# An attention kernel with a gated MLP: reciprocals stored in token order, and the first query product one slot earlier

## The chip, the cores and the metric

The kernel runs on one core of one Trainium2 chip. The metric is device time in microseconds of one execution; a span is the time from the first to the last instruction in the profile. Engine names are those of the profile: PE is TensorE's matmul, PEld its weight load, DVE VectorE, ACT ScalarE, POOL GpSimd, SP the SyncE queue that issues almost all DMAs here.

## The reference

```python
xn = layernorm(x)                       # x: 2048 tokens x 512
# A: attention, 32 heads of 128, keys and values from a cache of 2048 positions
q = (xn @ wq).reshape(B, Sq, H, Dh).transpose(0, 2, 1, 3)
p = softmax(q @ k_cache^T * Dh**-0.5)
s = (p @ v_cache).transpose(0, 2, 1, 3).reshape(B, Sq, H * Dh) @ wo
# B: shifted channel groups and an MLP
h = gelu(layernorm(xn) @ w1);  hs = shift(h) @ w2;  x1 = xn + hs
b = x1 + gelu(layernorm(x1) @ w3) @ w4
out = x + s * silu(b)
```

All arrays are bf16. The weights are wq 512 x 4096, wo 4096 x 512, w1 and w2 512 x 512, w3 512 x 1792, w4 1792 x 512.

## The kernel before

The MLP branch comes first (some 120 us); its end is interleaved with the first attention units. Attention is cut into 128 units: a unit is one head (`hh` within its group of four) for one quarter of the queries (512 tokens, `qt`), and eight groups `g` of four heads follow one another. Within a group the order is `qt`, then `hh`. Each unit has 8 slots (`SPU`), and one loop over `n` = 8 x unit + slot (line 921 on) writes down by hand, slot by slot, what is issued; `pin` keeps that order on every engine. `u` is the unit and `p` the slot (0 to 7).

**Scores and values.** In each slot `s_slot` makes the scores of two blocks of 128 keys against the 512 queries (two matmuls into one of two psS buffers), and ACT takes the exponential of both in one instruction (L423). `pv_run` follows ten slots behind (`LAG`): two matmuls per slot add values weighted by exponentials into `ps_o`, 128 head channels x 512 tokens, one of two psO buffers. A unit's value matmuls thus begin in slot 2 of the next unit, and need the buffer that the quotient (`norm`, L496) of the unit two before it has read.

**Softmax sums.** VectorE adds the exponentials of all keys in bf16 (`add_first` L429, `add_next` L434, `fold` L438, `fold_last` L442) down to 128 partitions x 512 tokens. For the first 124 units (`TURN`) the sums over the 128 partitions go this way: in slot 3 of the next unit SP issues a DMA transpose of that tile (`turn`, L467), so that partition `p` holds tokens `j*128 + p`, `j` = 0 to 3; in slot 0 of the unit after that VectorE adds along the free axis (`turned_sums`, L472) and takes the reciprocal (`turned_recip`, L478), 128 x 4 numbers; SP stores them to a small DRAM tile `dr` (L480); in slot 1 SP reads `dr` back, broadcast to all 128 partitions (`bcast`, L484), as `rb`, 128 x 512; in slot 7 VectorE multiplies `ps_o` by `rb` and writes `oT` (`norm`, L496). In `dr` the number of token `j*128 + p` stands at place `4p + j`. So `rb` and `oT` are in that order too: the quotient reads `ps_o` with a step of 128 numbers, and the projection's weight load picks 128 tokens of one block out of `oT` with a step of 4 (`o_cols`). The other four units have no such order: three of them use `sums`, whose `dr` is in token order, and the last is divided in halves in another way.

**Projection.** When the four heads of a group are done for a `qt`, `norm_queue` puts four token blocks on a list; each following unit takes one: four matmuls, one per head, into one psX buffer (tag `xm`), in the slots that `at_wo` names, and in the fifth of these VectorE adds the result to `sacc` (`wo_post`, L560).

**Queries.** From unit 16 on the queries of two heads are made together (a pair, `v` and `v + 1`) in seven products of two matmuls over 256 columns each, instead of eight (Strassen's way, in Winograd's form), during the 16 slots of units `v - 2` and `v - 1`. Products 1, 6, 2 go to one psX buffer (tag `xa`), products 7, 5, 4, 3 to the next one made from the same bank. ACT copies the buffer's first half after products 1 and 2 (`q_take` 0 and 1, L393), VectorE does the sums (`q_part`: L400, L403, L405, L407). `steps` names the slot of each, counted from the first slot of unit `v - 2`. In a slot the order is: scores, values, product, `q_take`, later the projection's matmul. The differences of weights that the products need come from `w_sum` (L361).

The slots that the change touches are set in these lines, with `FIRST` = 16 and `LAST` = 124:

```python
        for k, n in ((1, 1), (6, 2), (2, 5), (7, 8), (5, 9), (4, 12), (3, 13)):
            steps[a + n].append((product, v, k))
        for i, n in enumerate((1, 5)):
            steps[a + n].append((q_take, v, i))
...
        if FIRST - 2 <= u < LAST:
            at_wo = ([0, 3, 4, 6, 7], [0, 2, 3, 6, 7], [3, 4, 5, 6, 7], [0, 2, 3, 6, 7])[u % 4]
```

Of the kernel before, what the change touches and what calls it, by code (L numbers as in the profile page):

```python
# [10 lines left out]
FP32 = mybir.dt.float32  # L11
# [6 lines left out]
def kernel(  # L18
# [15 lines left out]
    nc = tc.nc  # L34
    P = nc.NUM_PARTITIONS
# [9 lines left out]
    QT = Sq // 512  # L45
# [5 lines left out]
    HG = 4  # L51
# [10 lines left out]
    pin = tc.keep_in_program_order  # L62

    def pool(name, bufs=1, space=None, **kw):
        if space is not None:
            kw["space"] = space
        return tc.tile_pool(name=name, bufs=bufs, **kw)
# [26 lines left out]
    drp = ent(pool("drp", 4, bass.MemoryType.DRAM))  # L94
# [16 lines left out]
    def mm(out, lhsT, rhs, start, stop, **kw):  # L111
# [9 lines left out]
        out=ident[:], in0=diag[:], scalar1=0.0, scalar2=None, op0=ALU.is_equal))  # L121
# [7 lines left out]
    TURN = range(NU - HG)  # L129
# [185 lines left out]
    def q_mm(u, dcs, tag="xa"):  # L315
        g, qt, hh = units[u]
        if dcs[0] == 0:
            st[u] = dict(psq=psX.tile([P, 512], FP32, tag=tag, name="ps_q"))
        for dc in dcs:
            mm(st[u]["psq"][:], wqs[g * HG + hh][:, dc, :],  # L320
               xnT[:, dc, qt * 512:(qt + 1) * 512], dc == 0, dc == DC - 1)
# [90 lines left out]
    def s_slot(u, p):  # L412
        g, qt, hh = units[u]
        s = st[u]
        sps = psS.tile([P, 2, 512], FP32, name="ps_s")
        for j in range(2):
            kc = 2 * p + j
            kv = kTs[g * HG + hh].rearrange("d (i p j) -> d i j p", p=P, j=KJ)
            mm(sps[:, j, :], kv[:, kc // KJ, kc % KJ, :], s["qT"][:], True, True)
        if p % 2 == 0:  # L420
            s.setdefault("pT", []).append(pB.tile([P, 4, 512], BF16, tag="pT", bufs=6, name="pT"))
        jj = 2 * (p % 2)
        pin(nc.scalar.activation(  # L423
            out=s["pT"][-1][:, jj:jj + 2, :], in_=sps[:], func=ACT.Exp, scale=SCALE))
# [7 lines left out]
    def add_next(u, i):  # L432
        a = st[u]["acc"]
        pin(nc.vector.tensor_tensor(out=a[:], in0=a[:], in1=st[u]["pT"][i][:], op=ALU.add))  # L434

    def fold(u):
        a = st[u]["acc"]
        pin(nc.vector.tensor_tensor(out=a[:, 0:2, :], in0=a[:, 0:2, :], in1=a[:, 2:4, :], op=ALU.add))  # L438

    def fold_last(u):  # L440
        a = st[u]["acc"]
        pin(nc.vector.tensor_tensor(out=a[:, 0, :], in0=a[:, 0, :], in1=a[:, 1, :], op=ALU.add))  # L442
# [26 lines left out]
    def turned_sums(u):  # L469
        s = st[u]  # L470
        sm = s["sm"] = smp.tile([P, 4], FP32, name="sm")
        pin(nc.vector.tensor_reduce(out=sm[:], in_=s["tT"][:], axis=mybir.AxisListType.X, op=ALU.add))  # L472

    def turned_recip(u):
        s = st[u]
        sm = s["sm"]
        rc = smp.tile([P, 4], FP32, name="rc")
        pin(nc.vector.reciprocal(out=rc[:], in_=sm[:]))  # L478
        s["dr"] = drp.tile([P, 4], FP32, name="dr")
        pin(nc.sync.dma_start(out=s["dr"][:], in_=rc[:]))  # L480

    def bcast(u):
        st[u]["rb"] = pB.tile([P, 512], FP32, tag="rb", bufs=2, name="rb")
        pin(nc.sync.dma_start(  # L484
            out=st[u]["rb"][:], in_=st[u]["dr"][:].rearrange("p j -> (p j)").partition_broadcast(P)))

    def norm(u):
        g, qt, hh = units[u]
        s = st.pop(u)
        if hh == 0:  # L490
            oTs[(g, qt)] = pB.tile([P, HG, 512], BF16, tag="oT", bufs=2, name="oT")
        o, rb, to = s["o"][:], s["rb"][:], oTs[(g, qt)][:, hh, :]
        if u in TURN:
            o = o.rearrange("k (j p) -> k p j", j=4)
            rb, to = (x.rearrange("k (p j) -> k p j", j=4) for x in (rb, to))
        pin(nc.vector.tensor_tensor(out=to, in0=o, in1=rb, op=ALU.mult))  # L496

    wo_box = {}
# [5 lines left out]

    def o_cols(g, qt, hh, ts):
        o = oTs[(g, qt)][:, hh, :]
        if (g * QT + qt) * HG + hh in TURN:
            return o.rearrange("k (p j) -> k j p", j=4)[:, ts, :]
        return o[:, ts * P:(ts + 1) * P]

    def wo_mm(g, t, hhs, tag="xm"):
# [28 lines left out]
    def pay():  # L540
        while owed:
            y_out(*owed.popleft(), nc.sync)
# [317 lines left out]
    def pv_run(n):  # L860
        while pv_at[0] <= n - LAG:
            pv_slot(*divmod(pv_at[0], SPU))
            pv_at[0] += 1
# [11 lines left out]
    def wo_slot(part, n, each=2, **kw):  # L875
        gg, t = wo_todo[0]
        if part < HG // each:
            wo_mm(gg, t, tuple(range(part * each, (part + 1) * each)), **kw)
            return
        wo_todo.popleft()  # L880
        wo_post(gg, t, n)
        if gg == NG - 1 and t % 4 < 3 and t + 1 not in fin and t // 4 not in LATE:
            fin_load(t + 1)
# [5 lines left out]
    first, third = {}, {}  # L889
    for v in pairs:  # L890
        a = (v - 2) * SPU
        for k, n in ((1, 1), (6, 2), (2, 5), (7, 8), (5, 9), (4, 12), (3, 13)):
            steps[a + n].append((product, v, k))
        for i, n in enumerate((1, 5)):
            steps[a + n].append((q_take, v, i))
        steps[a + 14].append((q_part, v, 3))
        first[v - 2] = v
        third[v - 1] = (v,)

    def fold_at(u):  # L900
        return 1 if u in third else 0

    def run_steps(n, which):
        for fn, v, k in steps.get(n, ()):
            if fn is which:
                fn(v, k)
# [4 lines left out]
    for h in range(HG, H, 2):  # L911
        u = (h // HG) * QT * HG + (-4, -2)[h % HG // 2]
# [8 lines left out]
    for n in range(UB * SPU):  # L921
        u, p = divmod(n, SPU)
        extra = len(wo_todo) > 1 and u in (2 * HG, 2 * HG + 1)
        if p == 0 and wo_box:
            wo_slot(4, n, each=1)
        s_slot(u, p)
        pv_run(n)
        for v, dcs in q_plan.get(n, ()):
            q_mm(v, dcs)
        run_steps(n, product)  # L930
        run_steps(n, q_take)
        if p == 0 and 1 <= u:
            if u - 2 in TURN:
                turned_sums(u - 2)
                turned_recip(u - 2)
            add_next(u - 1, 3)
        if p == 1 and u - 2 in TURN:
            bcast(u - 2)
        if p == fold_at(u) and 1 <= u:
            for v in third.get(u, ()):  # L940
                q_part(v, 1)
            fold(u - 1)
            for v in third.get(u, ()):
                q_part(v, 2)
            if u != UA and u not in first:
                fold_last(u - 1)
        if p == 2 and u in first:
            q_part(first[u], 0)
            fold_last(u - 1)
        if p == 3 and u - 1 in TURN:  # L950
            turn(u - 1)
        if p == 0:
            twice = extra
        if twice and p < 3:
            wo_slot(p, n, tag="xa")
        for v, k in ((u + 1, 3), (u + 2, 7)):
            if p == k and "psq" in st.get(v, ()) and (k == 3) == (v > FIRST):
                q_copy(v)
        if u - 2 in TURN:
            norm_p, sum_p, wo_p, each = 7, 5, 3, 1  # L960
        else:
            norm_p, sum_p, wo_p, each = 4, 5, 4, 1
        at_wo = [wo_p + i for i in range(HG // each + 1)]
        if FIRST - 2 <= u < LAST:
            at_wo = ([0, 3, 4, 6, 7], [0, 2, 3, 6, 7], [3, 4, 5, 6, 7], [0, 2, 3, 6, 7])[u % 4]
        if p == norm_p and 2 <= u and not u - 2 in TURN:
            norm_queue(u - 2)
        if p == sum_p and 1 <= u and u - 1 not in TURN:
            sums(u - 1)
        if p == sum_p + 1 and 1 <= u and u - 1 not in TURN:  # L970
            bcast(u - 1)
        if u == UA and p in (1, 2, 3):
            wo_slot(p - 1, n)
            if p == 3:
                fold_last(u - 1)
        if p in at_wo and wo_todo and pS is not None and (p == at_wo[0] or wo_box):
            wo_slot(at_wo.index(p), n, each=each)
        if p == norm_p and u - 2 in TURN:
            norm_queue(u - 2)
        run_steps(n, q_part)  # L980
        if p == 4:
            add_first(u)
        if p == 6:
            add_next(u, 2)
        pay()
        held_mm(n)
        for fn in todo.pop(n, ()):
            fn()
        if pS is None and not held:
            right.close()  # L990
            pS = right.enter_context(pool("pS", side="right", reuse_waits="tile"))
# [3 lines left out]
    n = UB * SPU  # L995
# [27 lines left out]
    def pv_to(k):  # L1023
# [29 lines left out]
        out=diag[:], in0=diag[:], scalar1=0.0, scalar2=None, op0=ALU.is_equal))  # L1053
# [98 lines left out]
```

## Time and profile before

| | us |
|---|---|
| median of 3 runs | 1241.74 |
| lowest and highest run | 1241.14, 1241.91 |
| the profiled execution | 1240.9 |
| its span | 1239.1 |
| TensorE's granted clock | 1.000 of full speed |
| ACT busy, DVE busy | 1112.6, 1030.3 |
| 16 DMA engines: share of the span that queue q1's packets took | 41.1% |

How to read the rows that follow. A row of a group gives the line, the engine, the operation, output and inputs, shapes and count; then busy time in us and the mean of one in ns; then the engine's idle time just before, and what ended it. A row of the timeline gives the start in us, the length in us, and the same names, with "xN" where neighbouring instructions of one kind are merged; matmuls are pipelined, so the length of a merged pair includes the draining of the last, and the pace is read from starts. A row of the chain gives start, length and what. A row of a window gives its ends, its length, and the busy time and count of PE, PEld, DVE, ACT and POOL, then the clock, the share of the DMA engines and GB/s. A row of DMA issues gives the kind, the count, the size and the median time in us from issue to landing. A row of waits gives who waited for whom, the total in us, how many times and the longest.

### The profile page before, as it was taken

To read this page: it belongs to the slowest core of one execution; us is meant where nothing else is said; L and a number is where in the kernel's file an instruction comes from. 1 tells how busy PE (TensorE), PEld (TensorE's weight loads), DVE (VectorE), ACT (ScalarE), POOL (GpSimd) and SP (SyncE) were. 2 spreads that over 40 slices of the span, in tenths; PEclk is the share of its full clock that TensorE was granted. 3 is DMA by queue.
4 is the path that set the end of the run, shared out by engine and by line. 5 is a ranking of instruction groups with operands and counts; after the bars stand their busy time and mean duration, and the time that the engine had idled before them with its cause. 6 is when DMAs were issued, how large, how long until landed. Compare 5 with 4: busy or idle time off the path is not lost.

```text
span 1239.1 us, 17537 instructions
## 1 busy us (share of the span) xinstructions
PE 1233.0 (100%) x6267; PEld 644.2 (52%) x6267; DVE 1030.3 (83%) x1647; ACT 1112.6 (90%) x1237; POOL 26.7 (2%) x75
## 2 busy tenths in 40 slices
PE   9999999999999999999999999999999999999998
PEld 6444444455555555555555555555555555555555
DVE  7712778898888888888889888888889999999997
ACT  6345999899999999999999999999999999999996
POOL 5300000000000000000000000000000000000000
PEclk9999999999999999999999999999999999999999
DMA  8760112554334423353243423443345435543332
GB/s 175 171 148 21 31 39 65 98 97 91 66 76 100 109 53 82 86 112 84 57 90 95 111 55 69 100 103 75 71 87 107 102 65 86 103 103 69 77 80 67
DMA packets 244056, 107.75 MB, mean 87 GB/s; under 512 B 194816, under 2 KB 227712, under 8 KB 243968
## 3 DMA queue, kind: packets, MB, share of 16 engines
q1 hardware_dynamic: 243408, 106.17, 41.1%
q8 instruction: 49, 0.80, 0.3%
q14 instruction: 39, 0.32, 0.1%
q10 hardware_dynamic: 560, 0.46, 0.1%
HBM read 67.50 MB, written 2.36 MB: 56 GB/s over the span
## 4 chain that ended last, share of the span: by engine, by line
PE 95%; DVE 3%; DMA 1%; ACT 1%; issue 0%; POOL 0%; DVEq 0%; ACTq 0%
PE ps_s L112 39%; PE ps_o L112 37%; PE ps_q L112 8%; PE ps_wo L112 8%; PE ps_m L112 2%; DVE acc L434 1%; ACT pT L423 1%; DMA rb<-dr 0%; DMA tT<-acc 0%; DVE sm L472 0%; DVE oT L496 0%; DMA xin<-in_A_x_dram 0%; PE ps_oh L112 0%; DMA dr<-rc 0%; DVE y L1014 0%
## 5 line engine op out<-in xcount | busy, mean ns | idle before, releaser
L423 ACT ACTIVATE pT<-ps_s 128x1024 bf16<-128x1024 f32 x1016 | 1019.8, 1025 | 54.4 <-PE ps_s L112 24.8
L112 PE MATMUL ps_s<-qT,kT 128*128 128x512 bf16 (+1 forms) x2064 | 609.0, 377 | 0.0
L112 PE MATMUL ps_o<-pT,vb 128*128 128x512 bf16 x1984 | 589.9, 379 | 0.0
L434 DVE TENSOR_TENSOR acc<-acc,pT 128x2048 bf16<-128x2048 bf16 x254 | 307.0, 1209 | 54.6 <-ACT pT L423 54.1
L112 PEld LDWEIGHTS <-kT 128*128 128x128 bf16 x2064 | 232.7, 113 | 147.4 <-issue 2.4
L112 PEld LDWEIGHTS <-vb 128*128 128x128 bf16 x1984 | 194.0, 98 | 216.9 <-issue 0.3
L429 DVE TENSOR_TENSOR acc<-pT 128x2048 bf16<-128x2048 bf16 x127 | 155.4, 1224 | 43.0 <-ACT pT L423 41.9
L112 PE MATMUL ps_wo<-wo_h,oT 128*128 128x512 bf16 x496 | 186.2, 379 | 0.0
L438 DVE TENSOR_TENSOR acc<-acc 128x1024 bf16<-128x1024 bf16 x127 | 87.4, 688 | 2.5
L496 DVE TENSOR_TENSOR oT<-ps_o,rb 128x512 bf16<-128x512 f32 x127 | 86.6, 682 | 1.5 <-DMA rb<-dr 1.2
L472 DVE TENSOR_REDUCE sm<-tT 128x4 f32<-128x512 bf16 x124 | 83.9, 677 | 2.0 <-DMA tT<-acc 2.0
L112 PEld LDWEIGHTS <-oT 128*128 128x128 bf16 x528 | 59.1, 112 | 49.5 <-issue 0.6
L112 PEld LDWEIGHTS <-wc 128*128 128x128 bf16 x440 | 42.9, 98 | 57.9 <-issue 12.7
L560 DVE TENSOR_TENSOR sacc<-ps_wo,sacc 128x512 f32<-128x512 f32 x96 | 65.7, 684 | 0.0
L112 PEld LDWEIGHTS <-wq_h 128*128 128x128 bf16 x398 | 38.9, 98 | 46.3
L112 PE MATMUL ps_q<-xnT,wq_h 128*128 128x256 bf16 (+1 forms) x288 | 61.1, 298 | 0.4 <-DVE sacc L548 0.4
L407 DVE TENSOR_TENSOR qT<-ps_q,tq 128x512 bf16<-128x512 f32 x55 | 38.0, 692 | 23.7 <-PE ps_q L112 23.5
L442 DVE TENSOR_TENSOR acc<-acc 128x512 bf16<-128x512 bf16 x127 | 53.0, 417 | 0.5
L293 ACT ACTIVATE h2T<-ps_s 128x1024 bf16<-128x1024 f32 x28 | 28.7, 1024 | 25.9 <-PE ps_s L112 25.9
L112 PEld LDWEIGHTS <-w_sb 128*128 128x128 bf16 x368 | 33.6, 98 | 29.6
L112 PE MATMUL ps_s<-xn2T,w_sb 128*128 128x512 bf16 x224 | 48.8, 379 | 0.0
L112 PE MATMUL ps_q<-xs,wc 128*128 128x256 bf16 x246 | 46.8, 271 | 0.0
(102 smaller groups left out, 586.4 us busy)
## 6 DMA issues: line engine op xcount, KB each, us to landing
rb<-dr SPq DMA_DIRECT2D x127, 256.0 KB, 3.9
vb<-in_A_v_cache_dram SPq DMA_DIRECT2D x62, 256.0 KB, 3.0
wq_h<-in_A_wq_dram SPq DMA_DIRECT2D x32, 128.0 KB, 3.1
wo_h<-in_A_wo_dram SPq DMA_DIRECT2D x32, 128.0 KB, 2.7
w_sb<-in_B_w_dram SPq DMA_DIRECT2D x8, 256.0 KB, 5.1
kT<-in_A_k_cache_dram SPq DMA_TRANSPOSE x128, 2.8
xl<-in_A_x_dram SPq DMA_DIRECT2D x16, 128.0 KB, 3.0
dr<-rc SPq DMA_DIRECT2D x127, 2.0 KB, 1.4
```

Source lines behind the costliest of these rows:

```text
L112: pin(nc.tensor.matmul(out=out, lhsT=lhsT, rhs=rhs, start=start, stop=stop, **kw))
L293: pin(nc.scalar.activation(out=h2[c, f][:], in_=ps[:], func=ACT.Gelu_apprx_tanh))
L407: pin(nc.vector.tensor_tensor(out=s["q"][:, 1:3, :], in0=ps[:], in1=s["u"][:].unsqueeze(1).to_broadcast([P, 2, 256]), op=ALU.add))
L423: pin(nc.scalar.activation(out=s["pT"][-1][:, jj:jj + 2, :], in_=sps[:], func=ACT.Exp, scale=SCALE))
L429: pin(nc.vector.tensor_tensor(out=s["acc"][:], in0=s["pT"][0][:], in1=s["pT"][1][:], op=ALU.add))
L434: pin(nc.vector.tensor_tensor(out=a[:], in0=a[:], in1=st[u]["pT"][i][:], op=ALU.add))
L438: pin(nc.vector.tensor_tensor(out=a[:, 0:2, :], in0=a[:, 0:2, :], in1=a[:, 2:4, :], op=ALU.add))
L442: pin(nc.vector.tensor_tensor(out=a[:, 0, :], in0=a[:, 0, :], in1=a[:, 1, :], op=ALU.add))
L472: pin(nc.vector.tensor_reduce(out=sm[:], in_=s["tT"][:], axis=mybir.AxisListType.X, op=ALU.add))
L496: pin(nc.vector.tensor_tensor(out=to, in0=o, in1=rb, op=ALU.mult))
L560: pin(nc.vector.tensor_tensor(out=sa, in0=ps[:], in1=sa, op=ALU.add))
```

## The change

Three things change, all in the attention loop.

1. `dr` becomes a tile of 4 x 128, and L480 stores through a rearranged view of it: the four numbers of a partition go to four places 512 bytes apart, so that `dr` is in token order. It is read back as before. The quotient of a turned unit no longer rearranges its operands, and `o_cols` takes 128 neighbouring columns.
2. Product 1 of a pair, and the copy `q_take` 0 behind it, stand in slot 0 of unit `v - 2` instead of slot 1.
3. In units 14 to 123, the projection's matmuls and its sum stand in slots 1, 3, 4, 6 and 7 of every even unit, instead of 0, 3, 4, 6, 7 (units 0, 4, 8, ...) and 3 to 7 (units 2, 6, 10, ...). Odd units keep 0, 2, 3, 6, 7.

```diff
         rc = smp.tile([P, 4], FP32, name="rc")
         pin(nc.vector.reciprocal(out=rc[:], in_=sm[:]))
-        s["dr"] = drp.tile([P, 4], FP32, name="dr")
-        pin(nc.sync.dma_start(out=s["dr"][:], in_=rc[:]))
+        s["dr"] = drp.tile([4, P], FP32, name="dr")
+        pin(nc.sync.dma_start(out=s["dr"][:].rearrange("j p -> p j"), in_=rc[:]))
...
         o, rb, to = s["o"][:], s["rb"][:], oTs[(g, qt)][:, hh, :]
-        if u in TURN:
-            o = o.rearrange("k (j p) -> k p j", j=4)
-            rb, to = (x.rearrange("k (p j) -> k p j", j=4) for x in (rb, to))
         pin(nc.vector.tensor_tensor(out=to, in0=o, in1=rb, op=ALU.mult))
...
     def o_cols(g, qt, hh, ts):
         o = oTs[(g, qt)][:, hh, :]
-        if (g * QT + qt) * HG + hh in TURN:
-            return o.rearrange("k (p j) -> k j p", j=4)[:, ts, :]
         return o[:, ts * P:(ts + 1) * P]
...
-        for k, n in ((1, 1), (6, 2), (2, 5), (7, 8), (5, 9), (4, 12), (3, 13)):
+        for k, n in ((1, 0), (6, 2), (2, 5), (7, 8), (5, 9), (4, 12), (3, 13)):
             steps[a + n].append((product, v, k))
-        for i, n in enumerate((1, 5)):
+        for i, n in enumerate((0, 5)):
             steps[a + n].append((q_take, v, i))
...
         if FIRST - 2 <= u < LAST:
-            at_wo = ([0, 3, 4, 6, 7], [0, 2, 3, 6, 7], [3, 4, 5, 6, 7], [0, 2, 3, 6, 7])[u % 4]
+            at_wo = ([1, 3, 4, 6, 7], [0, 2, 3, 6, 7])[u % 2]
```

## The prediction

> **What bounds the kernel now.** I read the page's first lines, then the chain that ended last, then the windows, and last the timeline of single slots.
>
> ```profile
> span 1239.1 us, 17537 instructions
> ...
> PE 1233.0 (100%) x6267; PEld 644.2 (52%) x6267; DVE 1030.3 (83%) x1647; ACT 1112.6 (90%) x1237; POOL 26.7 (2%) x75
> ...
> PE 95%; DVE 3%; DMA 1%; ACT 1%; issue 0%; POOL 0%; DVEq 0%; ACTq 0%
> ```
>
> TensorE is the bound: 95% of the chain is matmul. Its ends are modelled, so "100%" hides small holes; they are found from starts. The chain gives the pace where nothing waits, and the windows the length of two neighbouring query pairs (16 slots each):
>
> ```profile
> 45.63 24.17 PE ps_s L112 x112
> ```
>
> ```profile
> 592.57:609.92 17.35, 17.35 (x89) 9.05 (x87) 14.77 (x23) 16.62 (x20) 0.00 (x0) 1.00 0.28 62
> 609.92:626.89 16.97, 16.97 (x87) 8.93 (x86) 14.49 (x23) 16.30 (x20) 0.00 (x0) 1.00 0.37 78
> ```
>
> A matmul over 512 columns takes 24.17/112 = 0.2158 us of TensorE, one over 256 half of it. Four units hold 64 score, 64 value and 16 projection matmuls and 28 of the query products: 144 x 0.2158 + 28 x 0.108 = 34.10 us. The two windows are 34.32 us together: 0.22 us of holes in two pairs. The clock column is 1.00, so it is no throttling. ACT is busy (fourth pair of columns) for 16.62 and 16.30 us of them, close behind but partly overlapped. The timeline shows where the holes are:
>
> ```profile
> 592.45 0.59 PE L112 MATMUL ps_o<-pT,vb 128*128 128x512 bf16 x2
> 592.57 0.40 ACT L393 ACTIVATE tq<-ps_q 128x256 f32<-128x256 f32 x1
> ...
> 593.03 0.38 PE L112 MATMUL ps_q<-xs,wc 128*128 128x256 bf16 x2
> ```
>
> ```profile
> 609.88 0.59 PE L112 MATMUL ps_o<-pT,vb 128*128 128x512 bf16 x2
> 609.92 0.38 ACT L393 ACTIVATE tq<-ps_q 128x256 f32<-128x256 f32 x1
> ...
> 610.35 0.38 PE L112 MATMUL ps_q<-xs,wc 128*128 128x256 bf16 x2
> ...
> 610.56 0.59 PE L112 MATMUL ps_s<-qT,kT 128*128 128x512 bf16 x2
> ```
>
> Product 6 (slot 2) could start when the two value matmuls ahead of it have streamed, at 592.45 + 0.43 = 592.88 and 609.88 + 0.43 = 610.31. It starts at 593.03 and 610.35, each time 0.05 us after ACT's copy of the first half of the same psX bank (`q_take` 0) has ended (592.97, 610.30). So TensorE waits for that copy: 0.15 us in one pair, 0.04 us in the next, 0.19 of the 0.22 us.
>
> **The change, part by part.**
>
> *Product 1 and its copy one slot earlier.* The copy stands on ACT behind the exponential of its own slot; now it will stand behind slot 0's instead of slot 1's, about one slot (1.08 us) earlier, and end some 0.6 us or more ahead of product 6. Nothing is added; two matmuls and one ACT instruction change places with a neighbour. The hole goes in every pair.
>
> ```profile
> L393 ACT ACTIVATE tq<-ps_q x55: 377/402/416, 249.1 to 1177.4; 128x256 f32<-128x256 f32 x55
> ```
>
> 55 pairs at (0.15 + 0.04)/2 = 5.2 us; by the windows at most 0.22/2 x 55 = 6.1. I take 5.0. What would hold product 1 in slot 0 is its bank, last read by `q_part` 3 (L407) of the pair before:
>
> ```profile
> 605.54 0.69 DVE L407 TENSOR_TENSOR qT<-ps_q,tq 128x512 bf16<-128x512 f32 x1 [0.53 <-PE ps_q L112]
> ...
> 608.15 0.38 PE L112 MATMUL ps_wo<-wo_h,oT 128*128 128x512 bf16 x1
> ```
>
> L407 ends at 606.23; product 1 will take the place of this projection matmul, at 608.15: 1.9 us to spare. If that cover went, TensorE would stop for the rest. On ACT the copy now stands ahead of slot 1's exponential, which ends near 610.0 today (the copy is issued behind it) and some 0.3 us later then; the scores of slot 3, which need its buffer, start at 610.56 and could start 0.04 earlier. That leaves 0.2 us; less room than before, and what is short of it TensorE would wait.
>
> *Projection slots of even units, from 0,3,4,6 and 3,4,5,6 to 1,3,4,6.* The same matmuls. One small hole goes with it:
>
> ```profile
> L361 DVE TENSOR_TENSOR wc<-wq_h,wc 128x256 bf16<-128x256 bf16 x28 | 8.0, 285 | 0.0
> ```
>
> ```profile
> 950.91 0.68 DVE L560 TENSOR_TENSOR sacc<-ps_wo,sacc 128x512 f32<-128x512 f32 x1
> ...
> 951.14 0.59 PE L112 MATMUL ps_o<-pT,vb 128*128 128x512 bf16 x2
> ...
> 951.65 0.38 PE L112 MATMUL ps_wo<-wo_h,oT 128*128 128x512 bf16 x1
> ```
>
> The slot-0 projection could start at 951.14 + 0.43 = 951.57 and waits until L560 has emptied its bank (951.59): 0.08 us, where a weight difference (L361) came just ahead of L560 on VectorE. These 28 differences are four to each of seven head groups, and one of the four falls on this place: 7 x 0.08 = 0.5 us.
>
> *Quotients and projection weights without a step.*
>
> ```profile
> L496 DVE TENSOR_TENSOR oT<-ps_o,rb 128x512 bf16<-128x512 f32 x127 | 86.6, 682 | 1.5 <-DMA rb<-dr 1.2 <-PE ps_o L112 0.3
> ...
> L560 DVE TENSOR_TENSOR sacc<-ps_wo,sacc 128x512 f32<-128x512 f32 x96 | 65.7, 684 | 0.0
> ```
>
> The stepped quotient takes 682 ns, the unstepped sum over the same shape 684: nothing to gain. [...]
>
> ```profile
> L112 PEld LDWEIGHTS <-vb 128*128 128x128 bf16 x1984 | 194.0, 98 | 216.9 <-issue 0.3
> ...
> L112 PEld LDWEIGHTS <-oT 128*128 128x128 bf16 x528 | 59.1, 112 | 49.5 <-issue 0.6
> ```
>
> The stepped weight load takes 14 ns longer, but runs under the 216 ns of the matmul before it; cover gone, it would be 528 x 0.014 = 7.4 us.
>
> *The store of the reciprocals, in 512 pieces of 4 bytes instead of 128 of 16.* No instruction is added; each of 124 stores gets dearer by an amount d that the trace does not show.
>
> ```profile
> wq_h<-in_A_wq_dram SPq DMA_DIRECT2D x32, 128.0 KB, 3.1
> wo_h<-in_A_wo_dram SPq DMA_DIRECT2D x32, 128.0 KB, 2.7
> ...
> dr<-rc SPq DMA_DIRECT2D x127, 2.0 KB, 1.4
> ```
>
> The last column is the time to landing. wq_h's source lies in 512 runs, wo_h's in 128: 0.4 us for the same bytes. In the store itself (DMA view of 609.40 to 610.80, 40 slices of 0.035 us) the pieces move in six slices:
>
> ```profile
> DMA  0000000000000000000000026452100000000000
> ```
>
> 0.21 us; four times that is 0.63 more. Lower end 0 (a smaller count of pieces cannot be undercut by a larger one), upper end wq_h's whole landing, 3.1 - 1.4 = 1.7, far because it also moves 128 KB. I take d = 0.5, between the two rows that differ in pieces. [...]
>
> What waits for d is the loop store, broadcast (L484, behind the store's landing on SP), quotient, next sum, next store:
>
> ```profile
> 609.40 0.33 SPq L480 DMA_DIRECT2D dr<-rc  x1
> 610.81 0.33 SPq L484 DMA_DIRECT2D rb<-dr  x1
> 611.90 1.20 SPq L467 DMA_TRANSPOSE tT<-acc  x1
> ...
> 617.66 0.33 SPq L480 DMA_DIRECT2D dr<-rc  x1
> ```
>
> ```profile
> 616.15 0.68 DVE L496 TENSOR_TENSOR oT<-ps_o,rb 128x512 bf16<-128x512 f32 x1
> 616.75 0.67 DVE L472 TENSOR_REDUCE sm<-tT 128x4 f32<-128x512 bf16 x1
> ```
>
> ```profile
> 618.56 0.59 PE L112 MATMUL ps_o<-pT,vb 128*128 128x512 bf16 x2
> ```
>
> ```profile
> rb<-dr SPq DMA_DIRECT2D x127, 256.0 KB, 3.9
> ```
>
> ```profile
> DVE oT L496 <- DMA rb<-dr: 1.2, 2, 0.7
> ```
>
> The broadcast lands at 610.81 + 3.9 = 614.7, the quotient starts at 616.15 because VectorE gets to it then: 1.4 us of slack. Only 2 of 127 quotients wait for it today (the row of waits: 1.2 us, 2 times, 0.7 the longest). A later quotient holds TensorE only when the next unit's first value matmul (618.56) is reached, 1.7 us after it ends. Behind the broadcast on SP stands the transpose L467 at 611.90; SP is free from 611.14, so 0.5 us does not move it here. With d = 0.5 the store costs nothing.
>
> **Sum.** The profiled execution took 1240.9 us (1239.1 of span and 1.8 around it), 0.8 below the median of the runs. 1240.9 - 5.0 - 0.5 = 1235.4. Near the end VectorE has less room and may keep some of it:
>
> ```profile
> 1074.28:1177.39 103.11, 103.11 (x517) 53.99 (x515) 97.28 (x153) 98.72 (x110) 0.00 (x0) 1.00 0.39 84
> ```
>
> 94% busy (97.28 of 103.11) over the last six pairs; I give back 0.2 us of their 0.5. As a median: 1241.7 - 5.3 = 1236.4 us.
>
> **The rivals.**
>
> *The ring of reciprocals closes (slower).* Place: L480 to L484. From d = 1.4 on, the slack is used up, and each unit is longer by d - 1.4; the gain of 5.3 us is eaten at d = 1.4 + 5.3/124 = 1.44. At the far bound, 1.7: 124 x 0.3 = 37 us, 1241.7 - 5.3 + 37 = 1273; at 1.5, 1249. For it: two units in 127 wait already, the pieces are four times as many, and it recurs 124 times. Against: the rows that differ in pieces say 0.4 to 0.6.
>
> *The hole stays.* Product 6 could be held by something that ends with the copy by chance, or product 1 in slot 0 opens a hole of its own; then 1241.5. For it: ACT has only 0.7 us of idle time in a window of 17. Against: the same 0.05 us behind the copy in holes of different size, and the free bank 1.9 us early.
>
> *The steps count after all.* Loads of the projection weights are not fully hidden: 7.4 us more, 1229. Against it: the two windows leave 0.03 us of holes unexplained.
>
> **How the numbers follow.** What measurement can tell from no change here is about 0.2%, 2.5 us. Forecast 0.66, its own range 1234.8 to 1238.5; ring 0.17 (1244 to 1273); hole stays, or a d near 1.44 that just eats the gain, 0.14 (1239.5 to 1243); steps 0.03. Faster 0.66 + 0.03 = 0.69, same 0.14, slower 0.17. The range runs from 1234.5 (all holes gone, 6.1 + 0.5 and a little) to 1250, d = 1.5; what lies beyond it is most of the ring and the steps, under 2 in 10.
>
> **What would show it.** Right: product 6 starts 0.43 us after the value matmuls ahead of it, and two windows of a pair each sum to about 34.1 us; the store lands at 1.8 to 2.0 us; L496's idle time on rb stays under some 5 us in all; L496 still near 682 ns; loads from oT near 98 ns with no effect. Wrong: a store that lands after 2.8 us, and L496 waiting for rb in most units; or a hole ahead of product 1 in slot 0.

## The result, and the profile after

The changed kernel took 2151.5 us (median of 4 runs, 2146.9 to 2154.2), the kernel before 1241.8 (4 runs, 1241.1 to 1242.3): a ratio of 1.732, interval 1.729 to 1.735. The prediction was 1236.4 with a range up to 1250.

The page of the changed kernel: span, busy time, packets, the chain that ended last, and the groups and DMA issues that answer to those shown of before.

```profile
span 2145.1 us, 17537 instructions
...
PE 1501.7 (70%) x6267; PEld 692.5 (32%) x6267; DVE 1038.9 (48%) x1647; ACT 1107.3 (52%) x1237; POOL 26.9 (1%) x75
...
DMA packets 291672, 107.75 MB, mean 50 GB/s; under 512 B 242432, under 2 KB 275328, under 8 KB 291584
...
DMA 83%; DVE 9%; PE 7%; SPq 1%; issue 1%; ACT 0%; POOL 0%; DVEq 0%
...
L493 DVE TENSOR_TENSOR oT<-ps_o,rb 128x512 bf16<-128x512 f32 x127 | 87.8, 692 | 811.8 <-DMA rb<-dr 811.5
...
rb<-dr SPq DMA_DIRECT2D x127, 256.0 KB, 5.1
...
dr<-rc SPq DMA_DIRECT2D x127, 2.0 KB, 8.9
```

The bound has moved from TensorE (95% of the chain before) to DMA (83%). As many instructions run and as many bytes move; the packets were 244056 before, so 47616 = 124 x 384 more, as the change says. The store's landing went from 1.4 to 8.9 us. VectorE's quotient, which waited 1.2 us for the broadcast in the whole kernel before, now waits 811.5, and TensorE's value matmul waits behind that. By the table of waits it happens in nearly every unit (us in all, times, longest):

```profile
DVE oT L493 <- DMA rb<-dr: 811.5, 125, 9.3
PE ps_o L112 <- DVE oT L493: 637.5, 124, 7.5
```

One turn of the ring, from a store to the next, in SP's timeline and in VectorE's (start, duration, line; in brackets the idle time before and its releaser):

```profile
1000.41 0.38 SPq L480 DMA_DIRECT2D dr<-rc  x1
1009.26 0.33 SPq L484 DMA_DIRECT2D rb<-dr  x1
1009.68 1.20 SPq L467 DMA_TRANSPOSE tT<-acc  x1
...
1016.37 0.38 SPq L480 DMA_DIRECT2D dr<-rc  x1
```

```profile
1014.79 0.69 DVE L493 TENSOR_TENSOR oT<-ps_o,rb 128x512 bf16<-128x512 f32 x1 [7.16 <-DMA rb<-dr]
1015.44 0.69 DVE L472 TENSOR_REDUCE sm<-tT 128x4 f32<-128x512 bf16 x1
```

Store to broadcast 8.85 us (1000.41 to 1009.26), broadcast to quotient 5.5, quotient to next store 1.6: 15.96 us, where the rows of before had 8.26 between two stores. The broadcast itself lands 1.2 us later than before (5.1 for 3.9); the transpose L467 is now issued 0.42 us behind it, where there were 1.1 us in the rows of before. By the windows, one for each of two such turns, the whole kernel follows:

```profile
1000.21:1016.16 15.95, 10.53 (x45) 4.93 (x44) 7.03 (x11) 8.20 (x9) 0.00 (x0) 0.82 0.20 41
1016.16:1031.69 15.53, 10.85 (x43) 4.82 (x42) 7.73 (x12) 8.14 (x9) 0.00 (x0) 0.83 0.15 36
```

A unit takes 31.48/2 = 15.74 us, where two pairs of units took 34.32, so 8.58 a unit. 124 x (15.74 - 8.58) = 888 of the 910 us that the kernel lost.

What the store does in its 8.85 us is seen in the page of the window 1000.41 to 1009.61 alone (DMA's busy tenths in 40 slices of 0.23 us):

```profile
DMA  0000730000000000000000000000000000000000
...
DMA packets 528, 0.00 MB, mean 0 GB/s; under 512 B 528, under 2 KB 528, under 8 KB 528
```

528 packets are the 512 pieces and 16 more (in the same view of before 144, so 128 and 16). They move in two slices, between 0.92 and 1.38 us after the issue; then the 16 DMA engines are idle for 7.5 us, and only then does the store count as landed. Moving the pieces takes little; nearly all of the time lies behind the last of them. That is what the experiments are about.

### The profile page after: what moved, and what is told of

Read it like the earlier page. It is cut to its first block, busy times and chain, and to the rows that moved or that the text cites. A ratio compares the mean times of both kernels' runs of the same rounds, so it can differ in the third digit from the quotient of the medians.

```text
span 2145.1 us, 17537 instructions
## 1 busy us (share of the span) xinstructions
PE 1501.7 (70%) x6267; PEld 692.5 (32%) x6267; DVE 1038.9 (48%) x1647; ACT 1107.3 (52%) x1237; POOL 26.9 (1%) x75
## 4 chain that ended last, share of the span: by engine, by line
DMA 83%; DVE 9%; PE 7%; SPq 1%; issue 1%; ACT 0%; POOL 0%; DVEq 0%
DMA dr<-rc 54%; DMA rb<-dr 25%; DVE sm L472 4%; DVE oT L493 3%; PE ps_s L112 3%; DMA tT<-acc 3%; PE ps_o L112 2%; DVE rc L478 1%; PE ps_m L112 1%; PE ps_q L112 0%; SPq L144 0%; SPq L484 0%; SPq L467 0%; DVE acc L434 0%; PE ps_wo L112 0%
## 5 line engine op out<-in xcount | busy, mean ns | idle before, releaser
L112 PE MATMUL ps_o<-pT,vb 128*128 128x512 bf16 x1984 | 712.8, 447 | 619.4 <-DVE oT L493 619.4
L112 PE MATMUL ps_s<-qT,kT 128*128 128x512 bf16 (+1 forms) x2064 | 704.6, 428 | 0.1
L112 PEld LDWEIGHTS <-vb 128*128 128x128 bf16 x1984 | 214.2, 108 | 923.9 <-issue 766.2
L493 DVE TENSOR_TENSOR oT<-ps_o,rb 128x512 bf16<-128x512 f32 x127 | 87.8, 692 | 811.8 <-DMA rb<-dr 811.5
L112 PEld LDWEIGHTS <-kT 128*128 128x128 bf16 x2064 | 249.2, 121 | 222.6 <-issue 107.4
L112 PE MATMUL ps_wo<-wo_h,oT 128*128 128x512 bf16 x496 | 227.2, 462 | 0.0
L112 PEld LDWEIGHTS <-wc 128*128 128x128 bf16 x440 | 50.3, 114 | 75.6 <-issue 41.6
L112 PE MATMUL ps_q<-xs,wc 128*128 128x256 bf16 x246 | 59.9, 334 | 0.0
```

The costliest lines, as they stand in the source:

```text
L112: pin(nc.tensor.matmul(out=out, lhsT=lhsT, rhs=rhs, start=start, stop=stop, **kw))
```

## The experiments

Two theories of the late landing were set against each other. Theory A: a store lands late where many of its pieces fall close together in memory. Theory B: it lands late because it has many pieces. The expectations name a 64-byte line of DRAM as the place that pieces share, and let them be written there one behind the other; both were the author's assumption, and no run shows a border at 64 bytes or such an order. First the change was taken apart.

**e1_slots: only the slots (parts 2 and 3 of the change).**

```diff
-        for k, n in ((1, 1), (6, 2), (2, 5), (7, 8), (5, 9), (4, 12), (3, 13)):
+        for k, n in ((1, 0), (6, 2), (2, 5), (7, 8), (5, 9), (4, 12), (3, 13)):
...
-        for i, n in enumerate((1, 5)):
+        for i, n in enumerate((0, 5)):
...
-            at_wo = ([0, 3, 4, 6, 7], [0, 2, 3, 6, 7], [3, 4, 5, 6, 7], [0, 2, 3, 6, 7])[u % 4]
+            at_wo = ([1, 3, 4, 6, 7], [0, 2, 3, 6, 7])[u % 2]
```

> The slots alone: product 1 and its copy in slot 0, projection slots 1, 3, 4, 6, 7 in even units; store, quotient and weight loads as before. My forecast of this part stands: the holes ahead of product 6 (0.15 and 0.04 us by turns) and the seven of 0.08 us go, 1236.4 us, between 1235 and 1238. Rival (the hole stays): another wait takes their place, 1241 to 1242.

Measured: 1236.04 us (5 runs, 1235.3 to 1236.3) beside 1240.79 of the kernel before on that chip (15 runs); ratio 0.9960, 0.9947 to 0.9974. TensorE's timeline at a product 6:

```profile
590.66 0.59 PE L112 MATMUL ps_o<-pT,vb 128*128 128x512 bf16 x2
591.09 0.38 PE L112 MATMUL ps_q<-xs,wc 128*128 128x256 bf16 x2
```

591.09 is 590.66 + 0.43: no hole. And the length of two neighbouring pairs of units:

```profile
588.93:606.00 17.07, 17.02 (x87) 9.02 (x86) 14.62 (x23) 16.33 (x19) 0.00 (x0) 1.00 0.27 63
606.00:623.07 17.07, 16.96 (x86) 8.99 (x87) 14.62 (x23) 16.33 (x19) 0.00 (x0) 1.00 0.36 77
```

34.14 us in place of 34.32, with 34.10 worked out for no hole at all. The slots alone bring most of what the whole change was forecast to bring, 4.75 us of 5.3, and this version is faster than both kernels. Parts 2 and 3 were not run apart.

**e2_store: only the store, with quotient and weight loads without a step.**

```diff
-        s["dr"] = drp.tile([P, 4], FP32, name="dr")
-        pin(nc.sync.dma_start(out=s["dr"][:], in_=rc[:]))
+        s["dr"] = drp.tile([4, P], FP32, name="dr")
+        pin(nc.sync.dma_start(out=s["dr"][:].rearrange("j p -> p j"), in_=rc[:]))
...
-        if u in TURN:
-            o = o.rearrange("k (j p) -> k p j", j=4)
-            rb, to = (x.rearrange("k (p j) -> k p j", j=4) for x in (rb, to))
...
-        if (g * QT + qt) * HG + hh in TURN:
-            return o.rearrange("k (p j) -> k j p", j=4)[:, ts, :]
```

> The store in 512 pieces alone, with the quotients and weight loads that go with it; slots as before. If the ring of reciprocals is all of the loss, it is bound by the store's landing, and the slots are of no account: 2145 to 2160 us, store landing 8.9 us. If the slots add to the loss, it is clearly below 2140.

**e3_no_step: only the lines without a step** (the last two pieces of the diff above), the store as before. The quotients are divided by the sums of other tokens of the same unit.

> Quotients and weight loads without a step, store in 128 pieces of 16 bytes as before: the reciprocals then stand in another order than the tokens, so quotients are divided by other tokens' sums. Same instructions and shapes. If the step costs nothing, 1241.7 us within 0.1% (quotient 682 to 692 ns, weight load from oT 98 ns). Rival: weight loads were not hidden, 1234 us.

Measured: e3_no_step 1240.73 us (11 runs), ratio 1.0000, 0.9991 to 1.0008; e2_store 2026.25 (2 runs), ratio 1.633, 1.630 to 1.636. So the step is worth nothing, and the store alone makes a loss of this size. Groups of e3_no_step (mean ns of one after the comma):

```profile
L493 DVE TENSOR_TENSOR oT<-ps_o,rb 128x512 bf16<-128x512 f32 x127 | 86.6, 682 | 1.9 <-DMA rb<-dr 1.7
...
L112 PEld LDWEIGHTS <-oT 128*128 128x128 bf16 x528 | 51.3, 98 | 49.6 <-issue 0.7
```

The quotient takes the same 682 ns, the weight load 98 for 112, and the time does not change (1240.73 us for 1240.79). Landings in e2_store:

```profile
rb<-dr SPq DMA_DIRECT2D x127, 256.0 KB, 4.8
...
dr<-rc SPq DMA_DIRECT2D x127, 2.0 KB, 8.3
```

e2_store was 125 us faster than the changed kernel, though both have the ring. It had been expected at 2145 to 2160. The difference could be the slots, or the chip, since the two were measured on different chips.

**a2_changed_again and e2_store_again: the changed kernel and e2_store, unedited, on one chip.**

> The changed kernel as it is, on the same chip as the next run, since the store alone took 2026 us and the whole change 2151 on another chip. If the slots cost time once the ring binds, it is again some 125 us above the store alone; if the two chips differ in what a store takes to land, the two are within 1% of each other.

> The store alone, as before. If the two chips differ, both runs are near 2026 or near 2150; if the slots matter, this one is near 2026 and the other near 2150.

Measured on that chip: 2154.65 and 2156.15 us (2 runs each; before 1241.42), ratios 1.735 (1.730 to 1.740) and 1.736 (1.731 to 1.742), and the store landed in 8.9 us in both. So the slots are of no account once the ring binds, and the 125 us lay between the two measurements, on different chips: 0.6 us in the store and 0.3 in the broadcast (8.3 and 4.8 for 8.9 and 5.1), 124 x 0.9 = 112 of them.

**p1_pieces: a second store in each turned unit that nobody reads, in slot 5, in eight shapes by turns.** All leave `rc`, apart from pg, which leaves a zeroed tile.

```diff
+        if p == 5 and u - 2 in TURN:
+            probe(u - 2)
...
+    def probe(u):
+        rc, k = st[u]["rc"], u % 8
+        if k == 0:
+            t = drp.tile([P, 4], FP32, tag="pa", bufs=2, name="pa")
+            pin(nc.sync.dma_start(out=t[:], in_=rc[:]))
+        elif k == 1:
+            t = drp.tile([4, P], FP32, tag="pb", bufs=2, name="pb")
+            pin(nc.sync.dma_start(out=t[:].rearrange("j p -> p j"), in_=rc[:]))
+        elif k == 2:
+            t = drp.tile([P, 4, 16], FP32, tag="pc", bufs=2, name="pc")
+            pin(nc.sync.dma_start(out=t[:, :, 0], in_=rc[:]))
+        elif k == 3:
+            t = drp.tile([P, 1], FP32, tag="pd", bufs=2, name="pd")
+            pin(nc.sync.dma_start(out=t[:], in_=rc[:, 0:1]))
+        elif k == 4:
+            t = drp.tile([P, 16], FP32, tag="pe", bufs=2, name="pe")
+            pin(nc.sync.dma_start(out=t[:, 0:1], in_=rc[:, 0:1]))
...
```

> Before, with one more store per unit in slot 5 that nobody reads, of eight forms by turns; their time to landing is what counts. Theory A, pieces that share a 64-byte line of DRAM are written one after the other: 128 x 16 B 1.4 to 2.2 us; 512 x 4 B in token order (16 in a line) 8.9; 512 x 4 B, each in its own 64 B, about 2; 128 x 4 B in a row (16 in a line) about 8; 128 x 4 B each in its own 64 B 1.5; 256 x 8 B (8 in a line) about 5; 512 x 64 B about 2; 512 x 4 B spaced 8 B (8 in a line) about 5. Theory B, every small piece costs the same wherever it goes (7.5 us / 384 = 0.02 us each): 512 pieces of 4 B 8.9 in all three layouts, 128 x 4 B 1.4 to 2.5 in both, 256 x 8 B about 4, 512 x 64 B open. The kernel's own time should stay within 1% of before, unless a slow store holds up the loads behind it.

Landings in p1_pieces (KB each, median us from issue to landing). pa: 128 pieces of 16 bytes in a row. pb: 512 of 4 bytes in token order. pc: 512 of 4 bytes, one every 64 bytes. pd: 128 of 4 bytes in a row. pe: 128 of 4 bytes, one every 64 bytes. pf: 256 of 8 bytes in token order. pg: 512 of 64 bytes. ph: 512 of 4 bytes, one every 8 bytes.

```profile
pg<-zero SPq DMA_DIRECT2D x15, 32.0 KB, 2.4
...
pa<-rc SPq DMA_DIRECT2D x16, 2.0 KB, 2.2
pb<-rc SPq DMA_DIRECT2D x16, 2.0 KB, 9.7
pc<-rc SPq DMA_DIRECT2D x16, 2.0 KB, 2.9
pd<-rc SPq DMA_DIRECT2D x16, 0.5 KB, 8.1
pe<-rc SPq DMA_DIRECT2D x15, 0.5 KB, 2.3
pf<-rc SPq DMA_DIRECT2D x15, 2.0 KB, 4.7
ph<-rc SPq DMA_DIRECT2D x15, 2.0 KB, 4.8
```

Theory B falls twice: 512 pieces set apart land in 2.9 us (pc), and 128 pieces, as many as before the change, take 8.1 when they lie side by side (pd). The same 128 pieces set apart take 2.3 (pe). Theory A stands. The kernel's time did not come out as expected, though: 1364.44 us, a tenth longer, for stores that nothing waits for. The ordinary store beside them lands late now; SP's wait for it (us in all, times, longest) in p1_pieces, and before:

```profile
SPq L514 <- DMA dr<-rc: 383.5, 127, 9.1
```

```profile
SPq L484 <- DMA dr<-rc: 174.2, 127, 2.9
```

Here the ordinary store landed after a median of 2.8 us, against 1.4 before: slow stores held up what was issued behind them. p3_quiet, below, shows that in a single store (4.45 us for 1.41).

**e4_eight_bytes: half way, 256 pieces of 8 bytes.** `dr` is 2 x 128 x 2, and quotient and weight loads keep a step to match.

```diff
-        s["dr"] = drp.tile([P, 4], FP32, name="dr")
-        pin(nc.sync.dma_start(out=s["dr"][:], in_=rc[:]))
+        s["dr"] = drp.tile([2, P, 2], FP32, name="dr2")
+        pin(nc.sync.dma_start(out=s["dr"][:].rearrange("a p b -> p a b"),
+                              in_=rc[:].rearrange("p (a b) -> p a b", a=2)))
...
-            o = o.rearrange("k (j p) -> k p j", j=4)
-            rb, to = (x.rearrange("k (p j) -> k p j", j=4) for x in (rb, to))
+            o = o.rearrange("k (a b p) -> k a p b", a=2, b=2)
+            rb, to = (x.rearrange("k (a p b) -> k a p b", a=2, b=2) for x in (rb, to))
...
```

> Before, with the reciprocals stored in 256 pieces of 8 bytes (dr as 2 x 128 x 2), eight pieces to a 64-byte line, quotient and weight loads stepped to match. By the ring and by pieces that share a line: the store lands after about 4.4 us (4.7 in the probe, which had more traffic beside it), the broadcast after 3.9 to 4.8, and with 1.6 us for quotient, sum, reciprocal and issue a turn of the ring takes 10.1 to 10.8 us against 8.6 for a unit today: 124 x 1.5 to 2.2 = 190 to 270 more, 1430 to 1510 us. If the landing of the store did not set the pace, 1241.

Measured: 1361.79 us (2 runs), ratio 1.097, 1.094 to 1.100, faster than the 1430 to 1510 expected: the store landed after 3.6 us, where 4.4 had been assumed (4.7 in p1_pieces). Landings and the quotient's wait in e4_eight_bytes:

```profile
rb<-dr SPq DMA_DIRECT2D x127, 256.0 KB, 4.1
...
dr<-rc SPq DMA_DIRECT2D x127, 2.0 KB, 3.6
```

```profile
DVE oT L498 <- DMA rb<-dr: 195.0, 115, 5.4
```

With its own landings the ring gives 3.6 + 4.1 + 1.6 = 9.3 us a unit; the time gives 8.58 + (1361.8 - 1241.4)/124 = 9.55. For the changed kernel the same sum gives 8.9 + 5.1 + 1.6 = 15.6, and the windows 15.74. One sum of median landings holds, to 0.25 us, at two sizes of the cost: the ring sets the time. For e4_eight_bytes these 0.25 us are a quarter of what a unit lost, so the sum gives its size, not its last digit.

**p2_lines: eight more shapes as in p1_pieces** (pieces 32, 16 and 8 bytes apart, rows 512 bytes apart, 16-byte pieces, a store into SBUF, and two of before).

```diff
+        if k == 0:
+            t = drp.tile([P, 4, 8], FP32, tag="qa", bufs=2, name="qa")
+            pin(nc.sync.dma_start(out=t[:, :, 0], in_=rc[:]))
+        elif k == 1:
+            t = drp.tile([P, 4, 4], FP32, tag="qb", bufs=2, name="qb")
+            pin(nc.sync.dma_start(out=t[:, :, 0], in_=rc[:]))
...
```

> Before, with one more store per unit that nobody reads, as in the first probe, eight other forms. If a line is 64 bytes and its pieces are written one after the other at some 0.45 us each above the first: 512 x 4 B spaced 32 B (2 in a line) 2.5 to 3.5 us; spaced 16 B (4 in a line) 3 to 4; 4 pieces in the first 32 bytes of every 64 (4 in a line) 3 to 4; 4 pieces in the first 32 bytes of every 512, the same 3 to 4 (if the line were 512 bytes, less than the form before); 512 x 16 B in four rows (4 in a line) 3 to 4; 512 x 4 B into SBUF instead of DRAM about 2; token order again 9.5; 128 x 16 B in a row again 2.2. If only the smallness of the piece counts, the first four agree within 0.5 us.

1371.34 us. The trace has no landing of qc, qe, qf and qg, a single one of qa (3.3 us), qb (6.3) and qd (3.7), and 3.3 as the median of qh, the form of before, which had landed in 2.2 in p1_pieces; slow stores beside them may have drawn them out. It decides nothing; the shapes that mattered were repeated with few stores, far apart.

**p3_quiet: an extra store in slot 6 of units 4 to 6 of each 16 only**, 512 pieces of 4 bytes at a pitch of 64, 32, 16 and 8 bytes (pa to pd), in token order (pe), and 128 in a row (pf).

```diff
+        if p == 6 and 4 <= u % 16 < 7:
+            probe(u - 2, u % 16 - 4 + 3 * (u // 16 % 2))
...
+            name, step = ("pa", "pb", "pc", "pd")[k], (16, 8, 4, 2)[k]
+            t = drp.tile([P, 4, step], FP32, tag=name, bufs=2, name=name)
+            pin(nc.sync.dma_start(out=t[:, :, 0], in_=rc[:]))
...
```

> Before, with one more store that nobody reads in slot 6 of three units of each group of heads, where SP issues no loads; six forms, four samples each. 512 pieces of 4 B with 1, 2, 4, 8 and 16 to a 64-byte line, and 128 pieces of 4 B with 16 to a line. If what counts is how many pieces share a line: about 1.9, 2.4, 3.2, 4.7, 8.9 us, and 8 for the 128 pieces, at 0.45 us for each further piece. If the number of pieces counts: the first five equal, and the last a quarter of their excess over 1.4.

Landings in p3_quiet, with 1, 2, 4, 8, 16 and 16 pieces to each 64 bytes:

```profile
pa<-rc SPq DMA_DIRECT2D x4, 2.0 KB, 2.9
pb<-rc SPq DMA_DIRECT2D x4, 2.0 KB, 3.1
pc<-rc SPq DMA_DIRECT2D x4, 2.0 KB, 3.9
pd<-rc SPq DMA_DIRECT2D x4, 2.0 KB, 4.1
pe<-rc SPq DMA_DIRECT2D x4, 2.0 KB, 9.6
pf<-rc SPq DMA_DIRECT2D x4, 0.5 KB, 9.0
```

Each step towards more closely packed pieces lands later, but not in even steps: most of it comes between 8 and 16. The 24 stores cost the kernel 16.3 us (1257.83 for 1241.54, one run each). How they cost it is seen on SP behind one of the stores pe (start, duration, line):

```profile
591.57 0.57 SPq L491 DMA_DIRECT2D pe<-rc  x1
596.41 0.32 SPq L480 DMA_DIRECT2D dr<-rc  x1
600.86 0.32 SPq L498 DMA_DIRECT2D rb<-dr  x1
```

The broadcast goes out when the ordinary store has landed: 4.45 us after it was issued, where the rows of before had 1.41. The pe landed after 9.1 us, at 600.7. So the ordinary store, 128 pieces of 16 bytes as before, landed only when the slow store ahead of it had. It is not stores alone: a load of 128 KB (`xl`) issued 0.6 us behind another pe (1148.61) landed after 9.6 us, with a median of 3.6 for its kind in this run. Why they wait is not shown.

**p4_neighbours: is it the piece count, or who lies beside whom?** Same places; 128 pieces at a pitch of 4, 8, 16 and 64 bytes (pa to pd), and 512 pieces in four rows, each of which has neighbouring partitions at a pitch of 8 or 16 bytes (pe, pf).

```diff
+            name, step = ("pa", "pb", "pc", "pd")[k], (1, 2, 4, 16)[k]
+            t = drp.tile([P, step], FP32, tag=name, bufs=2, name=name)
+            pin(nc.sync.dma_start(out=t[:, 0:1], in_=rc[:, 0:1]))
...
+            name, step = ("pe", "pf")[k - 4], (2, 4)[k - 4]
+            t = drp.tile([4, P, step], FP32, tag=name, bufs=2, name=name)
+            pin(nc.sync.dma_start(out=t[:, :, 0].rearrange("j p -> p j"), in_=rc[:]))
...
```

> Before, with one more store that nobody reads, in the same quiet places as the last probe. It asks why 16 pieces in a line took 9 us where 8 took 4: there the 8 came from two partitions, the 16 from sixteen. 128 pieces of 4 B, one a partition, at a pitch of 4, 8, 16 and 64 bytes (16, 8, 4 and 1 in a 64-byte line); 512 pieces of 4 B in four rows at a pitch of 8 and 16 bytes (8 and 4 in a line, each from another partition). If the number in a line decides, with its step between 8 and 16: 9, 4, 3, 2.5 us, and 4 and 3 to 4. If it is that many partitions write one line: about 9, 5 to 6, 3 to 4, 2.5, and 6 and 4.

Landings in p4_neighbours:

```profile
pa<-rc SPq DMA_DIRECT2D x4, 0.5 KB, 8.5
pb<-rc SPq DMA_DIRECT2D x4, 0.5 KB, 3.8
pc<-rc SPq DMA_DIRECT2D x4, 0.5 KB, 2.9
pd<-rc SPq DMA_DIRECT2D x4, 0.5 KB, 2.5
pe<-rc SPq DMA_DIRECT2D x4, 2.0 KB, 4.3
pf<-rc SPq DMA_DIRECT2D x4, 2.0 KB, 3.4
```

This is what was expected if the number in a line decides. In these two runs 128 and 512 pieces of one density land within some 1 us of each other: 16 to each 64 bytes 8.5 to 9.6 us, 8 to each 3.8 to 4.3, 4 to each 2.9 to 3.9, one to each 2.5 to 2.9. And eight pieces in 64 bytes land alike whether two partitions sent them (p3_quiet's pd, 4.1) or eight did (pe, 4.3). So among the pieces of 4 bytes run here density decides, up to 8 to each 64 bytes. At 16 they always came from 16 partitions, and the two are not told apart. Nor is the size of a piece: 128 pieces of 16 bytes, four to each 64 bytes, land in 1.4 us (before) to 2.2 (p1_pieces' pa), in other slots. The 24 stores of this run, with four of the slow shape for eight in p3_quiet, cost nothing: 1240.68 us for 1241.06 (one run each). Left open: that 64 bytes are the unit (no run shows a border), whether pieces in one place are written one behind the other, what makes the jump between 8 and 16, and what happens in the idle 7.5 us. That the pieces of the slow shapes touch is not enough by itself: e4_eight_bytes' pieces touch, and land in 3.6 us.

## Why the prediction was wrong

**The step that failed** is the size of d: "I take d = 0.5, between the two rows that differ in pieces", with an upper end of 1.7. It measured 8.9 - 1.4 = 7.5 us. The rows chosen price the movement: the digit row shows how long pieces are on the engines, and `wq_h` differs in the runs that are *read*. The movement takes no more than was reckoned (two slices, up to 0.46 us, beside four times 0.21). What was left out is a growth of the time between the last piece and the landing: some 0.4 us in the digit row of before, 7.5 us now. Of the shapes run, only *writes* of single numbers into neighbouring places showed it at this size (medians of 8.1 to 9.7 us to landing). No row of the trace before has one, and an upper end taken from a read bounded nothing. The lower end, 0, was argued from the number of pieces; that more pieces never land earlier is not shown, and p1_pieces has 512 set apart landing in 2.9 us and 128 side by side in 8.1.

**The rival of the closing ring** was right in place (L480 to L484) and in its law, one unit longer by what d exceeds the slack; at d = 1.7 it gave 1273. With the d measured, its law gives 1241.7 - 5.3 + 124 x (7.5 - 1.4) = 1993 us; a broadcast that lands 1.2 us later adds 149 and makes 2142, beside 2151.5 measured. That second term was not in the prediction: it asked whether the later broadcast would move the transpose behind it on SP, and not whether the two, issued closer together, would share the DMA engines. That this is why the broadcast lands later was not tried, and e4_eight_bytes speaks against it: there too the transpose is issued some 0.4 us behind the broadcast, which lands after 4.1 us. The cause of the 1.2 us stays open. The rival's chance, 0.17, rested on the same 1.7; at any size that a store of this shape took in a run (medians of 8.3 to 9.7), no other case was left.

**The hole ahead of product 6 and the slot-0 holes:** right. e1_slots has no hole there, and its pairs are even at 17.07 us; 4.75 us came of 5.3. That its 1236.04 is so near the 1236.4 predicted is partly luck, since the kernel before took 1240.79 on that chip, 0.9 less than the forecast started from. In the changed kernel the same slots are worth nothing, as e2_store_again shows.

**The steps that cost nothing:** right. e3_no_step does without them: 682 ns as before, 98 for 112 ns in a weight load that is hidden, ratio 1.0000.

**What would show it wrong** named a store that lands after 2.8 us and L493 (L496 before) waiting for `rb` in most units. Both came: 8.9 us, and 125 of 127.

## What to carry to other kernels

Price a DMA on a closed loop by its landing (here store 8.9, broadcast 5.1 and 1.6 us for the rest give 15.6 of the 15.74 us of a unit), and allow for a part of a write's landing that no count of bytes, packets or busy engines shows (here 7.5 us behind the last piece); where the trace has no write of the same shape, its cost is unknown upwards, and the range has to say so. Work out beforehand at which cost the loop closes: here 1.4 us of slack in a loop passed 124 times, so every further microsecond costs 124. To turn small data around, leave the write in its pieces of 16 bytes (1.4 us to landing here, 8.9 in pieces of 4 in token order) and take the step in the compute engine's reading, where it cost nothing here (682 ns with it and without); look for what a write of closely packed single numbers holds back on its queue, even if nobody reads it (behind one, the ordinary store landed after 4.45 us for 1.41; 24 extra stores cost 16.3 us in p3_quiet and nothing in p4_neighbours); and where a change has several parts, measure them alone, since the good part here (e1_slots, 0.4% faster) was buried under the bad one.

## What the runs showed of the hardware

**TensorE at half pace behind 119 of 124 stalls.** TensorE's timeline in the changed kernel, from the end of one stall until the pace is back:

```profile
1015.54 1.01 PE L112 MATMUL ps_o<-pT,vb 128*128 128x512 bf16 x2 [5.42 <-DVE oT L493]
...
1016.77 1.06 PE L112 MATMUL ps_s<-qT,kT 128*128 128x512 bf16 x2
1017.63 1.06 PE L112 MATMUL ps_o<-pT,vb 128*128 128x512 bf16 x2
...
1020.66 0.59 PE L112 MATMUL ps_s<-qT,kT 128*128 128x512 bf16 x2
1021.09 0.59 PE L112 MATMUL ps_o<-pT,vb 128*128 128x512 bf16 x2
```

Two matmuls start 0.86 us after two others (1017.63 - 1016.77), so 0.43 each; at full pace it is 0.43 for two (1021.09 - 1020.66). By windows of 1 us the granted clock is 0.50 up to 1019.5, 0.62 in the next and 1.00 from 1020.5 on: half pace for some 4.7 us. The clock's mean in a unit is 0.82 and 0.83 (the windows above), in the whole span 0.835. The value matmul waited for the quotient 124 times, for 2.82 to 7.54 us. In the window from 0.5 to 1.5 us behind each of these stalls the granted clock is 0.50 in 119, 0.52 to 0.67 in four, and 1.00 in one, the shortest. Why the clock falls, and at which length of stall, is not shown. By the author's estimate it costs little time here, since TensorE runs out of work and waits for the next quotient all the same: the stall after this one was 4.68 us, and at full pace it would have been longer. "PE 1501.7" beside 1233.0 before goes with this, not with more work: both pages count 6267 matmuls, and a value matmul takes 447 ns for 379.

**The landing differed between chips.** The kernel before differed by 0.6 us between two chips (1240.79 and 1241.42), e2_store by 130 (2026.25 and 2156.15), with its store landing in 8.3 us on the one and in 8.9 on the other. The kernel bound by a loop of DMA landings showed a difference that the one bound by TensorE did not. Each of the two was measured on one occasion, so that chip and occasion are not told apart.
